# The first main slot's second unit turned by VectorE instead of TensorE

## The chip, the cores and the metric

The kernel runs on one core of one Trainium2 chip. The time is that of one execution on the device in microseconds (us), taken as the median of several runs; before the change it is 705.68 us. The core's engines have queues of their own: TensorE (PE; its weight loads have a row of their own, PEld), VectorE (DVE), ScalarE (ACT), GpSimd (POOL) and SyncE (SP), which only issues transfers here. Each engine takes its queue in order.

## What is computed

Linear attention with exponential features over 8 batches, 8 heads, 576 tokens and 64 columns a head; its output, 4608 tokens of 512 columns, goes through a mixture of eight experts, one expert a token, chosen by a router with a memory along the sequence:

```python
q_p, k_p = phi(q), phi(k)          # exp(x w - max), exp(-(x w - max))
kv = einsum('bhsf,bhsd->bhfd', k_p, v); z = sum(k_p, axis=2)
x = (q_p @ kv) / (q_p @ z + 1e-6)  # heads side by side: 512 columns
...
e = fresh_e if s == 0 or local_gate[b, s] < 0.5 else prev_e
h = maximum(x[b, s] @ w1[e], 0.0)  # 512 -> 1024
out[b, s] = p[e] * (h @ w2[e])     # 1024 -> 512
```

All of it is in 32-bit floats.

## The kernel before

The attention fills the first part of the span. Its tokens are written to DRAM (`xs`), sorted by expert into units of up to 128 tokens, and the experts work on slots: a slot is up to four units of one expert. There are two early slots of three units (`eslots`), which run while the last tokens are being sorted, and then the main slots, the first of which (`by_size[4][0]`) has four units.

For a slot, POOL gathers each unit's tokens from `xs` into an SBUF tile `xg`, tokens on the partitions (`gather_x`, L1302). Layer 1 needs them the other way round, features on the partitions, and in two parts: `xhi`, a rounded copy that ACT casts (L1410), and `xlo`, the rest that DVE subtracts (L1412), both in `parts`. Weights are split the same way: SP loads a piece `wraw`, ACT casts `whi` (L1249), DVE subtracts `wlo` (L1252). A product is three matmuls: high by high, high by low, low by high (L1416 to L1418; the first column block of layer 1 at L1463 takes all high parts of `x` first, and `xlo` last). Layer 1 runs over eight blocks of hidden columns, twelve matmuls each, into PSUM tiles `l1`; layer 2 over the units, 24 matmuls each, into `l2`. ACT scales each unit's result to `y` (L1533), and POOL writes it out by token number (L1537).

A unit is turned in one of two ways:

- `whole` (L1329): four PE transposes into a PSUM tile `tr` (L1335), then `parts` from PSUM. `tokens(..., late=True)` returns one such call a unit.
- `early_rows` (L1380): DVE transposes 32 x 32 blocks of the unit into `z` (L1386), then sixteen copies of 32 partitions x 128 put the blocks in their places, back into `xg` (`places`, four copies for each `j`, L1396), then `parts` from `xg` (`split`). It returns a list of six calls: the blocks, four times places, split. For a slot of four units the copies with odd `j` go to DVE and those with even `j` to ACT.

In the kernel before, the first main slot's unit 0 goes through `early_rows` and units 1, 2 and 3 through `whole`. This happens in layer 2 of the second early slot. `run` gives that layer a list of calls (`later`, second list), one for each pause; the pauses stand behind the first and the third column block of each of its three units. So in order: nothing; unit 0's blocks; `singles` (a step of the plan, in which POOL gathers the list rows of the single units at L937, and unit 0's four places); `parts` of `run` (unit 0's split, unit 1 whole); unit 2 whole; unit 3 whole; and behind the layer the last step of the plan (`more`), which has POOL clear a buffer (L968) and DVE and ACT unpack the list (L970 to L975).

The order of each engine's queue is fixed when the program is built. The framework goes through the instructions with estimated durations of its own and gives a free engine the instruction that is ready; among several, that which was written first. `past(engine)` and `issue_after(x)` add that an instruction comes behind another on its engine: `self.marks` keeps the last marked one, and `parts` marks its subtract on DVE and its cast on ACT. `last_low` is the last weight subtract that was written.

Of the kernel before, what the change touches and what calls it, by code (L numbers as in the profile page):

```python
# [82 lines left out]
class Kernel:  # L83
# [9 lines left out]
    def run(self):  # L93
        nc, tc, A = self.nc, self.tc, self.A
        act, dve = self.act, self.dve
        with ExitStack() as root:
# [38 lines left out]
            n = NBP * NHP * NC  # L135
# [63 lines left out]
            no = lambda: None  # L199
            m = []  # L200

            def ahead(k):
                s = self.by_size[4][0]
                self.gather_x(s, k, self.marks[self.act] if k else None)
                if k == 0:
                    self.coming.append(s)
                if k == 3:
                    m.append(self.early_rows(s, 0))
                    m.extend(self.tokens([s], True)[1:])
            a = [lambda k=k: ahead(k) for k in range(4)]  # L210

            def more():
# [10 lines left out]

            def parts():
                m[0][5]()
                m[1]()
            e, turn = self.eslots[1], []
            for k in range(2):
                turn.append(self.early_rows(e, k))
# [1 line left out]
            def both(*fs):  # L231
                def run():
                    for f in fs:
                        f()
                return run
            u, v = turn
            self.slots(self.eslots, soon=[[no, u[0], u[1], go, u[2], u[3], go, u[4], v[0], go, both(row, v[1]), row,
                                           both(row, v[2]), row, both(row, v[3]), both(row, v[4])],
                                          [no] * 9 + [read, both(a[0], step), a[1], step, a[2], step, a[3]]],
                       later=[[plan_row, u[5], row, row, v[5], 2, row, row, listed], [no, lambda: m[0][0](), singles, parts] + [lambda k=k: m[k]() for k in (2, 3)] + [more]])  # L240
            back.close()
            self.mid.close()
            self.open_rest(root)
# [1136 lines left out]
    def early_rows(self, s, k):  # L1380
        e, x = {}, s["xg"][k]

        def blocks():
            e["z"] = self.back2.tile([128, DM], F32, name="z", tag="kvs", bufs=3)
            with self.tc.issue_after(self.last_low.ins) if s["n"] == 4 else self.past(self.dve):
                self.marks[self.dve] = self.dve.transpose(e["z"].rearrange("p (c t) -> p c t", t=32),  # L1386
                                                          x.rearrange("p (c r) -> p c r", r=32))

        def places(j):
            z, to = e["z"].rearrange("p (a b t) -> p a b t", a=4, b=4), x.rearrange("p (a t) -> p a t", a=4)  # L1390
            g = slice(32 * j, 32 * j + 32)
            for b in range(4):
                q, engine = slice(32 * b, 32 * b + 32), self.dve if s["n"] == 4 and j % 2 else self.act
                with self.past(engine):
                    copy = engine.copy if engine is self.act else engine.tensor_copy
                    self.marks[engine] = copy(to[q, :, g], z[g, :, b, :])  # L1396

        def split():
            hi, lo = self.into(s)
            o = slice(k * 128, k * 128 + 128)  # L1400
            self.parts(s, hi, lo, o, x.rearrange("p (a t) -> p a t", a=4))
        return [blocks] + [lambda j=j: places(j) for j in range(4)] + [split]
# [320 lines left out]
```

## Time and profile before

| | us |
|---|---|
| median of 3 runs | 705.68 |
| lowest, highest | 705.52, 706.1 |
| the profiled execution | 706.37 |
| its span, first to last instruction | 704.6 |

The span is what the profile's views cover; 1.77 us of the profiled execution lie around it. TensorE was granted its full clock throughout (1.000 as the mean). A timeline row gives the start, the duration, the engine, the line, the operation, output<-input with shapes, how many instructions were merged, and in brackets the idle time before it with what ended it. Pipelined matmuls overlap: the pitch from start to start is what one costs.

### The profile page before, as it was taken

To read this page: it belongs to the slowest core of one execution; us is meant where nothing else is said; L and a number is where in the kernel's file an instruction comes from. 1 tells how busy PE (TensorE), PEld (TensorE's weight loads), DVE (VectorE), ACT (ScalarE), POOL (GpSimd) and SP (SyncE) were. 2 spreads that over 40 slices of the span, in tenths; PEclk is the share of its full clock that TensorE was granted. 3 is DMA by queue.
4 is the path that set the end of the run, shared out by engine and by line. 5 is a ranking of instruction groups with operands and counts; after the bars stand their busy time and mean duration, and the time that the engine had idled before them with its cause. 6 is when DMAs were issued, how large, how long until landed. Compare 5 with 4: busy or idle time off the path is not lost. (4 is left out here: it accounts for less than half of the span.)

```text
span 704.6 us, 22501 instructions
## 1 busy us (share of the span) xinstructions
PE 694.4 (99%) x9304; PEld 615.2 (87%) x9304; DVE 480.0 (68%) x941; ACT 416.9 (59%) x916; POOL 269.0 (38%) x534
## 2 busy tenths in 40 slices
PE   7999999999999999999999999999999999999996
PEld 6999999999999999989888988888987888878885
DVE  5798989889998996687757774535466743367230
ACT  4776676777678875843756656627276654256210
POOL 0211100341046576562445575423273836225101
PEclk9999999999999999999999999999999999999999
DMA  7765554555557756064847563445747697372001
GB/s 218 234 185 155 141 149 132 155 162 138 145 155 229 223 175 192 6 187 127 253 163 258 170 208 138 151 165 221 255 165 266 219 357 256 106 250 73 28 16 39
DMA packets 64921, 120.96 MB, mean 172 GB/s; under 512 B 7050, under 2 KB 45130, under 8 KB 64758
## 3 DMA queue, kind: packets, MB, share of 16 engines
q1 hardware_dynamic: 56528, 96.71, 43.4%
q0 software_dynamic: 7968, 22.59, 9.4%
q8 instruction: 74, 1.21, 0.7%
q14 instruction: 31, 0.25, 0.1%
q10 hardware_dynamic: 320, 0.20, 0.1%
HBM read 97.93 MB, written 21.80 MB: 170 GB/s over the span
## 5 line engine op out<-in xcount | busy, mean ns | idle before, releaser
L1252 DVE TENSOR_TENSOR wlo<-wraw,whi 128x1024 fp32r<-128x1024 f32 x80 | 97.0, 1228 | 40.5 <-ACT whi L1249 40.1
L396 ACT ACTIVATE kp<-sb 128x512 f32<-128x512 f32 x144 | 83.3, 623 | 50.4 <-DVE sb L393 46.5
L1416 PE MATMUL l<-whi,hh 128*128 128x512 f32 (+1 forms) x288 | 112.8, 392 | 0.0
L1417 PE MATMUL l<-wlo,hh 128*128 128x512 f32 (+1 forms) x288 | 112.4, 390 | 0.0
L1418 PE MATMUL l<-whi,hl 128*128 128x512 f32 (+1 forms) x288 | 112.3, 390 | 0.0
L1249 ACT CAST whi<-wraw 128x1024 fp32r<-128x1024 f32 x80 | 82.5, 1047 | 47.4 <-PE l L1418 25.8
L1416 PE MATMUL l<-xhi,whi 128*128 128x512 f32 (+5 forms) x308 | 108.4, 352 | 0.0
L1418 PE MATMUL l<-xhi,wlo 128*128 128x512 f32 (+5 forms) x308 | 108.1, 351 | 0.0
L1417 PE MATMUL l<-xlo,whi 128*128 128x512 f32 (+5 forms) x308 | 108.0, 351 | 0.0
L392 DVE TENSOR_REDUCE m<-pj 128x8 f32<-128x1024 f32 (+1 forms) x74 | 88.3, 1193 | 21.9 <-PE pj L385 19.9
L1368 POOL COPY xg<-z 32x128 f32<-32x128 f32 x216 | 79.8, 369 | 48.6 <-DVE z L1356 27.7
L1472 ACT ACTIVATE hh<-l 128x384 fp32r<-128x384 f32 (+4 forms) x88 | 44.8, 509 | 88.6 <-PE l L1463 52.9
L1473 DVE SCALAR_TENSOR_TENSOR hl<-l,hh 128x384 fp32r<-128x384 f32 (+4 forms) x88 | 50.7, 578 | 65.6 <-ACT hh L1472 65.1
L393 DVE TENSOR_TENSOR sb<-pj,m 128x1024 f32<-128x1024 f32 (+1 forms) x74 | 88.5, 1196 | 5.6
L385 PE MATMUL pj<-first,kq 64*128 64x128 f32 x1152 | 86.0, 290 | 4.2 <-DMA first<-in_first 3.6
L1537 POOL DMA_INDIRECT out<-y,p_tokm x31 | 36.6, 1181 | 132.0 <-DVE y L1531 125.7
L517 PE MATMUL nm<-kvs,qp 128*64 128x73 f32 x2304 | 86.3, 227 | 0.1
L420 ACT ACTIVATE qp<-pj 128x512 f32<-128x512 f32 x144 | 78.1, 596 | 9.7 <-PE pj L405 9.0
L385 PEld LDWEIGHTS pj<-first,kq 64*128 64x128 f32 x1152 | 72.0, 192 | 10.2 <-DMA first<-in_first 3.6
L517 PEld LDWEIGHTS nm<-kvs,qp 128*64 128x64 f32 x2304 | 79.1, 137 | 0.5 <-PE nm L517 0.2
L437 PE MATMUL kvp<-v,kp 128*64 128x65 f32 x2048 | 76.5, 226 | 0.1
L437 PEld LDWEIGHTS kvp<-v,kp 128*64 128x64 f32 x2048 | 66.9, 139 | 3.3 <-ACT kp L396 0.2
(282 smaller groups left out, 1071.1 us busy)
## 6 DMA issues: line engine op xcount, KB each, us to landing
wraw<-in_w1h SPq DMA_DIRECT2D x44, 512.0 KB, 5.6
wraw<-in_w2h SPq DMA_DIRECT2D x44, 512.0 KB, 4.5
kq<-in_kqT SPq DMA_DIRECT2D x47, 384.0 KB, 4.0
v<-in_va SPq DMA_DIRECT2D x48, 195.0 KB, 3.3
xs<-xo SPq DMA_DIRECT2D x48, 128.0 KB, 2.8
whi<-in_w2h SPq DMA_DIRECT2D x8, 512.0 KB, 6.9
wlo<-in_w2h SPq DMA_DIRECT2D x8, 512.0 KB, 8.1
xs<-xo SPq DMA_DIRECT2D x16, 192.0 KB, 2.2
```

The costliest lines, as they stand in the source:

```text
L385: self.last_pe = self.pe.matmul((q if j else t)[:, h, i % 2, j, :], kq[r, j, s], self.w2[r], start=True, stop=True)
L392: dve.tensor_reduce(m[:, a:a + n], x[:, s], AX.X, ALU.max, apply_absolute_value=True)
L393: self.last_dve = dve.tensor_sub(to[:, s], x[:, s], m[:, a:a + n].unsqueeze(2).broadcast_to([128, n, 128]))
L396: self.last_act = act.activation(kp[:, :, :, sg, :].rearrange("p c h f -> p h c f"), sb[:, :, :, 0], AF.Exp, scale=1.0 - 2 * sg)
L437: self.pe.matmul(t[r, sg, h], kp[:, h, sg, r], v[:, h], start=first and sg + h == 0, stop=last and sg + h == 2)
L517: self.last_num = self.pe.matmul(e["t"][r, c - c0, k], self.ch[i]["qp"][:, sg, h, q0 + r.start:q0 + r.stop], kvs[:, sg, k], start=sg == 0, ...
L1249: self.act.copy(hi, raw)
L1252: self.last_low = (low or self.dve).tensor_sub(lo[:, c], raw[:, c], hi.bitcast(F32)[:, c])
L1368: self.marks[engine] = copy(to[q, :, g], z[g, :, b, :])
L1416: mm(o, ah, bh, start=first, stop=False)
L1417: mm(o, ah, bl, start=False, stop=False)
L1418: self.last_pe = mm(o, al, bh, start=False, stop=last)
```

## The change

Unit 1 of the first main slot goes through `early_rows` as unit 0 does, and no longer through `whole`. Its blocks are turned in the same pause as unit 0's; its places are called in the pause of `parts`, behind unit 0's split; its split is called in the next pause, ahead of unit 2. For slots of four units the engine of a group of four copies comes from a table of two units by four groups: unit 0 has ACT, DVE, ACT, DVE as before, unit 1 has DVE for the first group and POOL for the other three.

```diff
@@ ahead(k), in run
                 if k == 3:
-                    m.append(self.early_rows(s, 0))
-                    m.extend(self.tokens([s], True)[1:])
+                    m.extend(self.early_rows(s, i) for i in (0, 1))
+                    m.extend(self.tokens([s], True)[2:])
@@ run
             def parts():
                 m[0][5]()
-                m[1]()
+                for f in m[1][1:5]:
+                    f()
+
+            def others():
+                m[1][5]()
+                m[2]()
...
-                       later=[[plan_row, u[5], row, row, v[5], 2, row, row, listed], [no, lambda: m[0][0](), singles, parts] + [lambda k=k: m[k]() for k in (2, 3)] + [more]])
+                       later=[[plan_row, u[5], row, row, v[5], 2, row, row, listed], [no, lambda: [m[k][0]() for k in (0, 1)], singles, parts, others, lambda: m[3](), more]])
@@ early_rows, places(j)
-                q, engine = slice(32 * b, 32 * b + 32), self.dve if s["n"] == 4 and j % 2 else self.act
+                q, engine = slice(32 * b, 32 * b + 32), self.act
+                if s["n"] == 4:
+                    engine = (self.act, self.dve, self.act, self.dve, self.dve, self.pool, self.pool, self.pool)[4 * k + j]
```

## Rows read from the trace of the kernel before

**Rows 1.** The page, part 1: busy us (share of the span) and instructions

```profile
PE 694.4 (99%) x9304; PEld 615.2 (87%) x9304; DVE 480.0 (68%) x941; ACT 416.9 (59%) x916; POOL 269.0 (38%) x534
```

**Rows 2.** Waits of PEld, 326 to 705 us: total, times, longest

```profile
PEld l L1429 <- issue: 8.0, 28, 0.4
...
PEld l L1463 <- ACT whi L1249: 0.8, 1, 0.8
```

**Rows 3.** Timeline of PE around unit 1's transposes (columns: see above)

```profile
336.81 0.39 PE L1417 MATMUL l<-wlo,hh 128*128 128x512 f32 x1
337.04 0.39 PE L1418 MATMUL l<-whi,hl 128*128 128x512 f32 x1
337.27 0.60 PE L1335 MATMUL tr<-first,xg 128*128 128x128 f32 x4
337.63 0.48 PE L1416 MATMUL l<-whi,hh 128*128 128x512 f32 x1
337.94 0.40 PE L1417 MATMUL l<-wlo,hh 128*128 128x512 f32 x1
```

**Rows 4.** Timeline of PE where the first main slot begins

```profile
347.58 1.07 PE L1463 MATMUL l<-xhi,whi 128*128 128x512 f32 x4
```

**Rows 5.** Timeline of ACT, 342 to 347 us

```profile
342.37 0.62 ACT L1410 CAST xhi<-xg 128x512 fp32r<-128x512 f32 x1
342.89 0.58 ACT L1410 CAST xhi<-tr 128x512 fp32r<-128x512 f32 x1
...
344.89 1.08 ACT L1410 CAST xhi<-tr 128x512 fp32r<-128x512 f32 x2
345.84 1.08 ACT L1249 CAST whi<-wraw 128x1024 fp32r<-128x1024 f32 x1
```

**Rows 6.** Timeline of DVE, 333 to 348 us

```profile
333.60 0.69 DVE L1386 STREAM_TRANSPOSE z<-xg 128x512 f32<-128x512 f32 x1
334.23 1.17 DVE L1252 TENSOR_TENSOR wlo<-wraw,whi 128x1024 fp32r<-128x1024 f32 x1
...
342.50 1.23 DVE L1252 TENSOR_TENSOR wlo<-wraw,whi 128x1024 fp32r<-128x1024 f32 x1 [1.09 <-ACT whi L1249]
343.64 0.68 DVE L1412 TENSOR_TENSOR xlo<-xg,xhi 128x512 fp32r<-128x512 f32 x1
...
345.03 1.23 DVE L1252 TENSOR_TENSOR wlo<-wraw,whi 128x1024 fp32r<-128x1024 f32 x1
346.17 1.28 DVE L1412 TENSOR_TENSOR xlo<-tr,xhi 128x512 fp32r<-128x512 f32 x2
```

**Rows 7.** Timeline of POOL, 328 to 346 us

```profile
328.05 0.95 POOL L1302 DMA_INDIRECT xg<-xs,p_tokm  x1 [0.30 <-issue]
...
336.44 1.02 POOL L1537 DMA_INDIRECT out<-y,p_toke  x1 [4.94 <-ACT y L1533]
...
340.29 1.87 POOL L937 DMA_INDIRECT lr<-lst,p_rih  x1 [0.31 <-issue]
344.34 1.04 POOL L1537 DMA_INDIRECT out<-y,p_toke  x1 [2.18 <-ACT y L1533]
```

**Rows 8.** DMA issues, 326 to 332 us: count, median us to landing

```profile
xg<-xs,p_tokm POOLq DMA_INDIRECT x4, 3.6
```

**Rows 9.** Timeline of DVE in the first main slot, 360 to 367 us

```profile
360.63 0.47 DVE L1368 COPY xg<-z 32x128 f32<-32x128 f32 x2
...
365.91 1.23 DVE L1252 TENSOR_TENSOR wlo<-wraw,whi 128x1024 fp32r<-128x1024 f32 x1 [1.80 <-ACT whi L1249]
```

**Rows 10.** Timeline of POOL in the first main slot, 360 to 368 us

```profile
360.09 2.57 POOL L1368 COPY xg<-z 32x128 f32<-32x128 f32 x8 [5.25 <-DVE z L1356]
363.92 3.70 POOL L1368 COPY xg<-z 32x128 f32<-32x128 f32 x8 [1.26 <-DVE z L1356]
```

**Rows 11.** The same groups by tile `z`: ns min/median/max, first to last start

```profile
L1368 POOL COPY xg<-z x8: 281/286/288, 360.1 to 362.4; 32x128 f32<-32x128 f32 x8
...
L1368 POOL COPY xg<-z x8: 283/288/1349, 363.9 to 367.3; 32x128 f32<-32x128 f32 x8
```

## The prediction

> **What bounds the kernel now.** I read the page's busy times first: TensorE (PE) is busy for 99% of the span, every other engine for 68% or less [rows 1]. So a change counts only by what it takes from PE or by what it makes PE wait for. The waits of PE's weight loads from 326 us to the end say whether PE waits anywhere behind the place of the change: 28 short gaps inside one kind of small slot, and single waits of at most 0.8 us [rows 2]. A shift of PE's queue at 337 us will thus travel to the end of the span nearly whole.
>
> Then the timeline of PE. The four transposes of the second unit stand between two matmuls of the second early slot's layer 2 [rows 3]; the same pattern stands twice more, for the third and fourth units. Layer 1 of the first main slot begins on PE at 347.58 without a gap [rows 4]; its products with the low parts `xlo` come eight matmuls of 0.23 later, at 349.4. Its first matmul takes all 512 columns, so it needs `xhi` of all four units. The timelines of the other engines show how much time is left: ScalarE (ACT) casts the first unit's `xhi` at 342.37, the second's, out of PSUM, at 342.89, and has the last two done at 345.97 [rows 5]; VectorE (DVE) has the last `xlo` at 347.45 [rows 6]; GpSimd (POOL) sits idle until 336.44, then issues one output and three gathers up to 342.16, then an output at 344.34 [rows 7].
>
> **What is removed.** From the matmul at 337.04 to the second one behind the transposes at 337.94 are 0.90 us, where two pitches of 0.23 (336.81 to 337.04) would be 0.46 [rows 3]: the four transposes cost PE 0.44 us. Nothing covers that, so it is the gain. Layer 1 of the main slot would be wanted at 347.58 - 0.44 = 347.14. A PSUM tile is no longer used; nothing in the trace waits for one here, and I count it at nothing, whichever way.
>
> **What is added, on DVE.** One block transpose of 0.69 (pitch 0.63), right behind the first unit's at 333.60 [rows 6]. Its data, gathered second of four, are in SBUF by then (landing 3.6 us after issue, before 333) [rows 8]. It pushes the weight subtract at 334.23 and the first unit's copies back by 0.63. Behind those DVE idles until its next weight casts are ready, and the pieces of weights that it splits here belong to the slot that begins at 347, so I cost this at nothing; without that cover it would be 0.63. Four copies (two take 0.47, so 0.235 each [rows 9], 0.94 in all) are written behind the first unit's `xlo`, which ends at 344.32 [rows 6]: they end at 345.3 at the earliest. The second unit's `xhi` can't be cast before, 2.4 us later than now. The cast itself reads SBUF instead of PSUM, 0.62 for 0.58 [rows 5]; it is on ACT, beside PE.
>
> **What is added, on POOL.** Twelve copies, of which the trace has no case here. The nearest rows are eight of the same shape in a main slot: 2.57 us alone, a pitch of 0.32, and 3.70 where a weight subtract of DVE (two SBUF inputs, 365.91) ran beside them [rows 10]; there one copy of 288 ns became 1349 [rows 11]. So a weight subtract that is met costs 1.13.
>
> Where do they stand in POOL's queue? The blocks are ready at 333.60 + 0.63 + 0.69 = 334.92, and POOL idles until 336.44 [rows 7]: about four copies of 0.32 fit in front of the output, if the queue is built in the order in which things become ready. The output and the gathers were written earlier in the program and go first once they are ready, so the other eight copies come behind the last gather: 342.46 + 2.57 = 345.0 at the least. In that stretch DVE runs a weight subtract at 342.50, the first unit's `xlo` (its two inputs are in SBUF too) at 343.64, and another weight subtract, now behind the four copies at about 345.3. The bounds for the end of the copies: 345.0, or below that if more than four come first, and 346.3 + 1.13 + 0.68 + 1.13 = 349.2 with all twelve behind the gathers and all three held. I take eight copies and the first two holds, 345.0 + 1.13 + 0.68 = 346.8, and half of the third, as the pattern of one held copy per subtract is the nearest row: 347.4. The cast of 0.62 then ends at 348.0, against 347.14 wanted: PE waits 0.9.
>
> Queued behind the copies on POOL are the output at 344.34 [rows 7], the singles' list, which needs the buffer of that output, and the gathers for the next slot. They slide by up to 3 us. The next slot begins 192 matmuls of 0.23 us, 44 us, behind the main slot's start. What DVE and ACT do for the singles' list stands in front of their reads of the main slot's PSUM tiles; of those there are four, each filled by 12 matmuls (2.8 us), so three more are there to be filled, 8 us. That is the cover, and I cost the slide at nothing; without it PE would wait up to the 3 us.
>
> A page of the Trainium skill speaks against the change at one point more. Rows first: in the group of eight POOL copies at 360.09 two DVE copies ran at 360.63 [rows 9], and the POOL copies took 281 to 288 ns each [rows 11]; no hold is seen. "SBUF — State Buffer", section "Who interferes with whom", says that VectorE and GpSimd share a port pair as an exclusive lock, and that a VectorE `copy` in a two-port mode takes it too, not only a `tensor_tensor` with two SBUF inputs. By the rows the four DVE copies cost POOL nothing; by that rule they would hold POOL's for four times 0.235.
>
> **The sum.** -0.44 + 0.86 = +0.42 us. The profiled execution took 706.37 (span 704.6 and 1.77 around it), 0.69 more than the median of the three runs; with the change it would take 706.8, and the median 705.68 + 0.42 = 706.1. A difference of 0.2%, 1.41 us, is about what a measurement of this kernel can tell from none, so this is no change.
>
> **The rivals.**
>
> *In time.* The copies end before 346.5: because more than four go in front of the output, or because DVE's subtracts fall between them. For it: POOL idles 4.94 us before the output [rows 7], and bare copies end at 345.0. Against it: the blocks are ready only in the last 1.5 us of that idle time, and three subtracts stand in the way. Then only the gain is left: 705.68 - 0.44 = 705.24.
>
> *ACT held in its queue (slower).* ACT works in order. If the second unit's cast is queued in front of the casts of the third and fourth units (it is written before them), they all wait for POOL. They are now done at 345.97 [rows 5]; behind a cast that ends at 348.0 their 1.08 gives 349.1, and a weight cast between them another 1.08 [rows 5]. PE waits 1.9 to 3.0, the net is +1.5 to +2.6: 707.2 to 708.3. It decides for slower once the last cast ends behind 347.14 + 0.44 + 1.41 = 348.99. For it: that order of writing. Against it: at 345 the other two are ready and the second unit isn't, and a queue built by readiness would let them pass.
>
> *DVE's copies hold POOL's too.* Four holds of 0.235 on top of the forecast: 706.1 + 0.9 = 707.0. Against it stands the 281 to 288 ns [rows 11]. For it: only two DVE copies ran there. The page named above is the one that has this rule.
>
> *The queues come out otherwise further on.* The order of all queues is fixed at build time; a shift of half a microsecond can swap neighbours later. PE has no waits of size there [rows 2], so it can hardly gain, and lose about a microsecond: 704 to 707.5.
>
> *The change doesn't remove what it says.* PE's transposes are issued by one helper, and the second unit's call is dropped from the list; I give that no chance.
>
> **How the numbers follow.** Forecast (a PE wait of 0.3 to 1.5; 705.5 to 706.8) 0.47; in time 0.24; ACT held 0.14; DVE's copies too 0.08; further on 0.07. The likeliest is 706.1. The range from 705.0 to 707.5 holds the forecast, the case in time with a margin of 0.2, the copies' case and the lower third of ACT held; outside are the rest of it and half of the last case, some 0.13. Slower by over 0.2% (above 707.09): ACT held, half of the copies' case, an edge of the forecast and a part of the last: 0.22. Faster by over 0.2% (below 704.27): only a part of the last, 0.03. Within: 0.75.
>
> **What would show it.** Right: eight transposes by PE in front of the main slot instead of twelve; two block transposes back to back at about 333.6; some POOL copies in front of the first output, the others behind the third gather, some of them over 1 us long; ACT idle before the second unit's cast; a gap on PE in front of the first main matmul of about 0.9, released by that cast. Wrong: no gap there (the case in time); the third and fourth units' casts behind the second's (ACT held); or a difference in time that arises behind 370 us.

## The result and the profile after

The changed kernel takes 715.06 us, the median of four runs (714.48 to 716.69), against 705.6 for the kernel before, the median of four runs on the same chip (704.48 to 706.1). The ratio is 1.0134, with an interval from 1.0118 to 1.0149. That is 9.5 us slower, where the prediction had 0.4 us and a range that ended at 707.5. The profiled execution took 714.94 us, with a span of 713.2.

The first view is again the timeline of TensorE (PE); its columns are the start, the time, the engine, line and operation, the tiles, and in brackets the idle time before it with what ended it. Line 1470 of the changed kernel is line 1463 of the one before, 1423 to 1425 are 1416 to 1418. These rows are from the end of the second early slot on.

```profile
345.24 0.39 PE L1425 MATMUL l<-whi,hl 128*128 128x512 f32 x1
353.21 2.04 PE L1470 MATMUL l<-xhi,whi 128*128 128x512 f32 x4 [7.58 <-ACT whi L1254]
355.05 1.91 PE L1470 MATMUL l<-xhi,wlo 128*128 128x512 f32 x4
356.76 1.91 PE L1470 MATMUL l<-xlo,whi 128*128 128x512 f32 x4
358.46 0.63 PE L1423 MATMUL l<-xhi,whi 128*128 128x512 f32 x1
358.89 0.52 PE L1424 MATMUL l<-xlo,whi 128*128 128x512 f32 x1
359.25 0.39 PE L1425 MATMUL l<-xhi,wlo 128*128 128x512 f32 x1
```

Where the main slot began without a gap before [rows 4], PE now stands still for 7.58 us. And the first twelve matmuls behind the stop take 358.46 - 353.21 = 5.25 us. Before they took 350.30 - 347.58 = 2.72. The table of windows says why: the granted clock (the column `PEclk`, the third from the right) is 0.50 there, the lower of the two levels, 1.2 GHz in place of 2.4. It comes back to 1.00 in the stretch from 358.5 to 360 (0.78 as the mean): the matmuls from 359.25 on have the pitch of before. Each row gives the stretch, its length, then the busy time and the instructions of PE, PEld, DVE, ACT and POOL.

```profile
340.00:345.50 5.50, 5.50 (x29) 4.33 (x26) 3.99 (x7) 3.49 (x5) 4.58 (x4) 1.00 0.85 289
345.50:353.20 7.70, 0.13 (x1) 0.02 (x1) 1.43 (x3) 2.08 (x4) 1.53 (x3) 0.72 0.41 109
353.20:356.00 2.80, 2.79 (x7) 2.22 (x8) 2.40 (x4) 0.81 (x3) 0.69 (x2) 0.50 0.26 97
356.00:358.50 2.50, 2.50 (x8) 1.92 (x7) 0.18 (x1) 0.69 (x3) 1.89 (x3) 0.50 0.81 197
358.50:360.00 1.50, 1.50 (x7) 1.23 (x6) 0.60 (x1) 0.60 (x1) 1.20 (x2) 0.78 1.01 393
360.00:362.00 2.00, 2.00 (x10) 1.64 (x9) 0.09 (x1) 0.24 (x1) 0.45 (x1) 1.00 1.00 410
```

Who held PE? The timeline names the weights, which came last by a little. Followed back one step on ScalarE (ACT), where rows 5 had no wait, they stand in its queue behind the casts of `xhi`, and those behind a wait of 7.61 us for GpSimd (POOL). VectorE (DVE) subtracts `xlo` behind that cast.

```profile
342.93 0.58 ACT L1417 CAST xhi<-tr 128x512 fp32r<-128x512 f32 x1
351.12 0.62 ACT L1417 CAST xhi<-xg 128x512 fp32r<-128x512 f32 x1 [7.61 <-POOL xg L1403]
351.64 0.58 ACT L1417 CAST xhi<-tr 128x512 fp32r<-128x512 f32 x1
352.12 1.05 ACT L1254 CAST whi<-wraw 128x1024 fp32r<-128x1024 f32 x1
```

POOL itself (the answer to rows 7):

```profile
333.40 5.39 POOL L1403 COPY xg<-z 32x128 f32<-32x128 f32 x11 [3.50 <-DVE z L1391]
339.07 1.70 POOL L1544 DMA_INDIRECT out<-y,p_toke  x1 [0.28 <-POOL xg L1403]
341.08 1.82 POOL L942 DMA_INDIRECT lr<-lst,p_r  x1 [0.31 <-issue]
343.20 0.90 POOL L942 DMA_INDIRECT lr<-lst,p_rih  x1 [0.30 <-issue]
344.40 1.28 POOL L942 DMA_INDIRECT lr<-lst,p_rih  x1 [0.31 <-issue]
350.80 0.29 POOL L1403 COPY xg<-z 32x128 f32<-32x128 f32 x1 [5.11 <-DMA lr<-lst,p_rih]
```

Eleven of the twelve copies went in front of the output. The twelfth, 0.29 us long, stands behind the output and the three gathers of the singles' list, and the row says that it waited 5.11 us until the last gather had landed. It doesn't read what that gather brings: the gathers fill `lr`, the copy moves a block from `z` to `xg`. Its line of code asks for no such order; in the built program its wait is on the completion of every one of the four transfers that stand before it in POOL's queue. Whether the chip needs that wait, or only the program asks for it, no run here shows.

A trace could have told this beforehand. The tile view of `z` in the kernel before, POOL's copies alone, gives the idle time in front of them by what ended it. This group isn't among the rows ahead of the prediction, and I hadn't read it as a price:

```profile
L1368 POOL COPY xg<-z x216: 279/287/1349, 360.1 to 643.9; 32x128 f32<-32x128 f32 x108
...
  DVE z L1356: 27.7, 16
...
  DMA out<-y,p_tokm: 8.4, 4
```

Four times, 8.4 us in all, a POOL copy had waited for an output, which it has no business with either.

**An account by stages.** Single runs of the kernel before spread by 4 us (704.19 to 708.6 in 22 runs), and the profiles show where: the second early slot, which lies in front of the change's effects, began anywhere from 311.19 to 314.23 in the twelve profiled executions. So each trace is cut at the first matmul of a slot, the rows of PE that follow (before, then after; the main slot's own rows are in rows 4 and above):

```profile
312.80 0.87 PE L1463 MATMUL l<-xhi,whi 128*128 128x384 f32 x4
422.98 1.08 PE L1463 MATMUL l<-xhi,whi 128*128 128x512 f32 x4
502.30 0.74 PE L1463 MATMUL l<-xhi,whi 128*128 128x320 f32 x4
```

```profile
311.19 0.87 PE L1470 MATMUL l<-xhi,whi 128*128 128x384 f32 x4
431.52 1.08 PE L1470 MATMUL l<-xhi,whi 128*128 128x512 f32 x4
510.84 0.74 PE L1470 MATMUL l<-xhi,whi 128*128 128x320 f32 x4
```

Stage A runs from the second early slot to the first main slot (347.58 - 312.80 = 34.78 before), stage B from there over two main slots (422.98 - 347.58 = 75.40), stage C over the next two (79.32). Each figure is from the one profiled execution of its kernel. The table has the difference to the kernel before in each stage, their sum, and what the timed runs gave by their ratio to the kernel before on the same chip (the interval in us). The runs below stand in it too.

| kernel | A | of it, layer 2 | B | C | sum | timed |
|---|---|---|---|---|---|---|
| changed kernel | +7.24 | +7.25 | +2.91 | 0 | +10.2 | +9.5 (8.3 to 10.5) |
| e1_last_dve | +0.72 | +0.65 | +0.30 | 0 | +1.0 | +2.0 (1.0 to 3.0) |
| e2_first | +0.83 | +0.50 | +0.78 | +0.51 | +2.1 | +2.8 (1.7 to 3.8) |
| e3_behind | +4.94 | +4.57 | +1.96 | 0 | +6.9 | +7.5 (5.6 to 9.4) |
| e4_no_turn | -0.22 | -0.50 | 0 | 0 | -0.2 | +0.1 (-1.1 to 1.3) |
| e5_busy | +6.84 | +6.84 | +0.12 | 0 | +7.0 | +7.6 (6.1 to 9.1) |
| e6_swap | +0.16 | +0.03 | +0.85 | +0.75 | +1.8 | +2.0 (0.8 to 3.2) |
| e7_list | +0.34 | +0.35 | +0.10 | 0 | +0.4 | +0.7 (-0.4 to 1.8) |
| e8_late | +2.18 | +1.62 | +0.09 | 0 | +2.3 | +2.2 (0.9 to 3.5) |
| e9_all | +0.12 | +0.13 | +0.12 | 0 | +0.2 | -0.1 (-1.4 to 1.1) |
| e10_all_act | -0.28 | -0.27 | +0.12 | 0 | -0.2 | +0.5 (-0.6 to 1.7) |

The column "of it, layer 2" counts stage A only from the first layer 2 matmul of the second early slot, 18.11 us before the main slot in the kernel before:

```profile
329.47 0.39 PE L1416 MATMUL l<-whi,hh 128*128 128x512 f32 x1
```

The part of stage A ahead of that matmul lies before everything that the change or an edit moves. It took 16.66 to 16.80 us in eight of the executions, but 16.95 in e4_no_turn, 17.00 in e2_first, 17.04 in e3_behind and 17.23 in e8_late, where PE's weight load stands still for 0.3 to 0.6 us near 319.5 (in three of the four for DVE's `hl`). So the column is the better measure of what an edit does to stage A.

The sum lies inside the timed interval in every line. For the changed kernel, A is the stop less the transposes, 7.58 - 0.44 = 7.14 and 0.10 more; B is the lower level, 5.25 - 2.72 = 2.53 in the first twelve matmuls and the rest in the next ones.

### The profile page after: what moved, and what is told of

Same layout as the page of the kernel before. It is cut to its first block, busy times and chain, and to the rows that moved or that the text cites. A ratio compares the mean times of both kernels' runs of the same rounds, so it can differ in the third digit from the quotient of the medians.

```text
span 713.2 us, 22512 instructions
## 1 busy us (share of the span) xinstructions
PE 695.6 (98%) x9300; PEld 615.3 (86%) x9300; DVE 483.4 (68%) x946; ACT 417.8 (59%) x916; POOL 277.8 (39%) x546
```

## The experiments

In the code and in the expectations the units count from 0, so that unit 1 is the second one, which the change turns, and unit 2 the third. The theory: one copy behind transfers of POOL's own costs the stop, and the stop costs TensorE its level. The rivals: that POOL's copies are too many or too slow wherever they stand; that the lower level is only a companion; that the change has further costs in ACT's and DVE's queues or later on.

**The twelfth copy on DVE.**

```
...
-                     engine = (self.act, self.dve, self.act, self.dve, self.dve, self.pool, self.pool, self.pool)[4 * k + j]
+                     engine = (self.act, self.dve, self.act, self.dve, self.dve, self.pool, self.pool, self.pool)[4 * k + j] if (k, j, b) != (1, 3, 3) else self.dve
```

> The changed kernel with one of the sixteen copies moved: the twelfth of GpSimd's, the last, goes to VectorE; eleven stay on GpSimd. Theory A (one copy behind the gathers): the whole loss comes from that one copy, which stands behind one output and three gathers in GpSimd's queue and waits for them to land (5.1 us idle in the trace), and from the lower TensorE clock behind the gap. Then it is gone: 705.2 us (the kernel before at 705.7, less 0.44 for four transposes), no gap on TensorE in front of the first main slot. Theory B (GpSimd's work as such: twelve copies beside VectorE's subtracts are too slow, the mechanism of the forecast): eleven copies are nearly the same work, at least 713. Theory C (the second unit's cast holds ScalarE's queue wherever its copies are made): 708 or more.

708.34 us (707.06 to 708.55), ratio 1.0028 (1.0014 to 1.0043). One copy of 0.29 us moved, and 6.5 of the 7.24 us of stage A are gone, and 2.6 of the 2.91 of stage B with them. The eleven copies that stay cost little. But the time is not theory A's 705.2; it lies where theory C had it. What is left is a stop of 0.98 us, which the row puts down to DVE and not to ACT's queue (e6_swap, below, tries that):

```profile
347.95 1.17 PE L1470 MATMUL l<-xhi,whi 128*128 128x512 f32 x4 [0.98 <-DVE xlo L1419]
```

**All twelve in front.** POOL's copies are issued at a higher priority, so that none stands behind the output.

```
- with self.past(engine):
+ with self.past(engine), self.tc.high_priority() if engine is self.pool else nullcontext():
```

> The changed kernel with all twelve copies on GpSimd, but given priority over what else is ready, so that all twelve stand in front of the output and the three gathers in its queue. Only the place of one copy differs. Theory A: 705.2 us, no gap on TensorE; the output and the gathers 0.3 us later. Theory B: the same work on the same engine, so 714 to 716. Theory C: 708 or more.

708.94 us (706.86 to 710.28), ratio 1.0039 (1.0024 to 1.0054). Again the big stop is gone, without taking a copy from POOL: it is the place, not the engine. In the built program the queues of PE, ACT and DVE are those of the changed kernel; only POOL's differs, by the place of the twelfth copy. But 2 to 3 us remain (again the time of theory C), and they lie in three stages. In the main slot PE's weight loads waited 0.6 us for ACT's `hh` and 0.4 us for DVE's `hl`, where its layer 2 begins, 26.9 us behind its start (375.86):

```profile
375.34 0.39 PE L1425 MATMUL l<-whi,hl 128*128 128x512 f32 x1
375.86 0.50 PE L1423 MATMUL l<-whi,hh 128*128 128x512 f32 x1
```

The singles' list comes late too, on ACT 6.2 us behind the slot's start, where the kernel before had it 2.8 us behind (350.39). But the `hh` that are queued right behind it made PE wait for nothing. What is late at 375.86 is the work on the next slot's tokens, which stands on ACT and DVE between the `hh` and `hl`, and it is late because POOL's gathers of those tokens stand behind the list's memset, which had waited for an output to land:

```profile
353.96 0.30 POOL L973 MEMSET y<- 32x256 f32 x1 [4.26 <-DMA out<-y,p_toke]
358.63 0.95 POOL L1307 DMA_INDIRECT xg<-xs,p_tokm  x1 [0.30 <-issue]
```

The last of these gathers goes 9.67 us behind the slot's start, against 6.31 in the kernel before. The runs are in that order: where it goes at 8.2 us or earlier and the clock holds, stage B has at most 0.12 more than before; at 9.33 (e1_last_dve) it has 0.30, at 9.67 0.78, at 9.73 (e6_swap) 0.85.

**All twelve behind.** POOL's copies wait for the issue of the last gather.

```
- ins = pool.indirect_dma_start(...
+ ins = self.last_lr = pool.indirect_dma_start(...
...
- with self.past(engine):
+ with self.tc.issue_after(self.last_lr.ins) if engine is self.pool else self.past(engine):
```

> The changed kernel with all twelve copies behind the last of the three gathers in GpSimd's queue. Theory A: the first of them waits for the landing as the one copy did, and then twelve at a pitch of 0.32 us follow instead of one, 3.5 us more: 717 to 719 us, and a gap on TensorE of about 11 us. Theory B (no wait for a landing, only work and VectorE's holds): the copies end at 346.3 to 349.2, so 706 to 709.

713.34 us (711.83 to 714.53), ratio 1.0106 (1.0079 to 1.0133): slower than before, but less so than the changed kernel, which neither number had foreseen. POOL shows why. With no copies in front, the last gather goes 28.2 us behind the start of the second early slot (340.94 - 312.78), where the changed kernel has 33.2. The first copy still comes only 5.7 us behind that gather's start, and the twelve take 5.16, so the last is done 0.9 us earlier than in the changed kernel. The row names no transfer for this wait; in the built program it is again on the completion of the four in front. But ACT had cast the third and the fourth unit by then, and only one cast stood between the copies and PE.

```profile
340.94 1.59 POOL L942 DMA_INDIRECT lr<-lst,p_rih  x1 [0.31 <-issue]
346.64 5.16 POOL L1403 COPY xg<-z 32x128 f32<-32x128 f32 x12 [4.11 <-issue]
```

PE's stop is 4.92 us, ended by the cast of the second unit. So the price of the place isn't a fixed one: it is the landing of the last transfer in front, and whatever had delayed that transfer.

**The unit not turned at all.** The block transpose and the copies of the second unit are left out, which shows what the removal on PE is worth by itself.

```
  if k == 3:
      m.extend(self.early_rows(s, i) for i in (0, 1))
+     m[1][0:5] = [no] * 5
```

> The changed kernel without the turning of the second unit: its block transpose and its sixteen copies are left out, and its cast reads the rows as they were gathered. It shows what taking four transposes from TensorE is worth when nothing is put in their place: 705.2 us if the 0.44 us arrives at the end, 705.7 if it is lost on the way. If it were slower than 706, the loss would lie in the new order of the calls and not in the copies at all.

706.78 us (704.64 to 707.76), ratio 1.0002 (0.9985 to 1.0019). Stage A is 0.22 us shorter, half of the 0.44. But it holds a wait of 0.3 us for DVE's `hl`, which the kernel before doesn't have:

```profile
319.86 0.19 PEld L1424 LDWEIGHTS l<-xhi,whi 128*128 128x128 f32 x1 [0.31 <-DVE hl L1481]
330.39 0.39 PE L1424 MATMUL l<-whi,hh 128*128 128x512 f32 x1
```

It lies ahead of layer 2, where nothing has been edited. From layer 2 on the stage is 0.50 us shorter (348.00 - 330.39 = 17.61 against 18.11): the whole of the 0.44 arrives. By timing it can't be told from nothing.

**TensorE kept at work.** Thirty matmuls into a tile that nobody reads are put in the stop of the changed kernel.

```
+ def busy():
+     w = self.by_size[4][0]["w"][0][0]
+     t = self.pskv.tile([128, 512], F32, name="idle", tag="kvp")
+     for k in range(30):
+         with self.here():
+             self.last_pe = self.pe.matmul(t, w[:, 0:128], w[:, 0:512], start=True, stop=True)
...
-     ... others, lambda: m[3](), more]])
+     ... others, lambda: m[3](), both(more, busy)]])
```

> The changed kernel, with 30 matmuls of 128x128x512 added that TensorE works through while it would otherwise stand still ahead of the first main slot (they write a PSUM tile that nobody reads; nothing else is touched). Theory A (the still stretch also costs TensorE its level: the twelve first-layer matmuls behind it took 5.25 us against 2.72 before, and the slot's next ones about 0.4 more): the twelve take 2.7 to 2.9 us, the granted clock from 346 to 360 is 1.00, the stretch from the first matmul of the main slot to the first of the next is 43.5 us and not 46.4, and the time falls by 2.5 to 2.9 us, to about 712.3. Theory B (the clock is a mere companion, the twelve matmuls were slow because their operands came late): they still take about 5 us and the time stays at 715. In both, the first matmul of the main slot still comes some 42 us behind the slot before it.

713.4 us (712.31 to 713.91), ratio 1.0108 (1.0087 to 1.0129). The first main matmul still comes 41.62 us behind the slot before it (42.02 in the changed kernel), on operands just as late, but the level holds and stage B is 75.52 us, not 78.31:

```profile
346.81 6.96 PE L234 MATMUL idle<-whi 128*128 128x512 f32 x30
354.18 1.17 PE L1477 MATMUL l<-xhi,whi 128*128 128x512 f32 x4 [0.41 <-ACT whi L1261]
355.19 1.08 PE L1477 MATMUL l<-xhi,wlo 128*128 128x512 f32 x4
```

So 2.8 us of the loss are TensorE's level; work that has no use at all gains them back. In time the two kernels differ by 1.7 us between medians, less than the stage, and their intervals overlap a little.

**DVE's order.** e1_last_dve, with unit 2's subtract ahead of unit 1's.

```
  def others():
-     m[1][5]()
      m[2]()
+     m[1][5]()
```

> As e1_last_dve (the twelfth copy on VectorE), but VectorE subtracts unit 2's part ahead of unit 1's. Theory A (what was left of the stop ahead of the main slot, 0.98 us, is VectorE's order: the PSUM tile of unit 2 is given back only behind unit 1's subtract): the stop shrinks by one subtract, 0.6 us, to 0.3 to 0.4 us; from the slot before to the main slot 34.9 us against 35.5 in e1_last_dve and 34.8 before; the time falls by 0.6 us. Theory B (unit 1's cast, which comes at 345.4, or the weights set the stop): the stop stays at 0.9 to 1.0 us and the time at that of e1_last_dve.

707.66 us (705.87 to 710.01), ratio 1.0028 (1.0012 to 1.0045). The stop before the main slot falls from 0.98 to 0.36 us, stage A from +0.72 to +0.16 (from layer 2 on, +0.65 to +0.03), as expected: the PSUM tile of the third transpose, which the main slot's first matmul is to write, was given back a subtract too late (its reader is the third unit's `xlo`, which the row names). But the time doesn't fall, since stages B and C go up by 0.55 and 0.75: the main slot comes 0.6 us sooner, POOL's gathers for the next slot only 0.2, and the waits are those of e2_first.

```profile
PEld l L1423 <- ACT hh L1479: 0.6, 1, 0.6
PEld l L1425 <- DVE hl L1480: 0.4, 1, 0.4
```

**The singles' list in a tile of its own.** e2_first, but the list is unpacked in a tile that the output isn't still reading.

```
- t = (self.back2.tile([128, DM], F32, name="z", tag="kvs", bufs=3) if engine is dve else
+ t = (self.back2.tile([128, DM], F32, name="z", tag="kvs", bufs=3) if engine is dve or n == ONES + DUALS else
       self.mx2.tile([128, DM], F32, name="y"))
```

> As e2_first (all twelve copies ahead of the output), but the singles' list is unpacked in a tile of its own, so that its memset no longer waits for the second unit's output to land (4.26 us idle on GpSimd in e2_first). Theory A (the waits inside the main slot, 0.6 us for a ScalarE hh and 0.4 us for a VectorE hl, come of this list, whose copies stand ahead of the hh casts on ScalarE's queue at 355.2): ScalarE's list copies come at 349 to 352, the waits inside the main slot go, from the first matmul of the main slot to the first of the next 43.5 us against 44.3 in e2_first, and the time falls by 0.8 us or a little more. Theory B (the list has no part in them): 44.3 us as before, and the time of e2_first.

706.99 us (705.54 to 708.56), ratio 1.001 (0.9995 to 1.0025). Stages B and C fall back to +0.10 and 0 from +0.78 and +0.51, and the waits inside the slots are gone. So the list is their cause, but not by the way of theory A: ACT's list copies come at 353.96, not at 349 to 352, as the gathers' landing takes the place of the output's, and that is still 5.7 us behind the slot's start (6.2 in e2_first). What moves is POOL. No memset waits there, and the last gather for the next slot goes 5.35 us behind the slot's start, not 9.67:

```profile
353.62 0.95 POOL L1307 DMA_INDIRECT xg<-xs,p_tokm  x1 [0.30 <-issue]
```

The lag is handed on to the third main slot on the same queue: in the second one a group of POOL's copies waited 4.48 us for an output in e2_first and 1.08 in e7_list, and the last of the gathers behind them went 73.9 us behind the first main slot's start, not 67.0. That path is read from the rows; no run tries it alone.

**The gathers behind the twelfth copy.**

```
  def singles():
-     more()
      ...
  def others():
+     more()
```

> The changed kernel, with the three gathers of the singles' list issued behind the twelfth copy; GpSimd's queue is now eleven copies, the output, the twelfth copy, the second output, the gathers. Theory A (the twelfth copy waited for the landing of the gathers in front of it): it now waits for the output alone, issued at about 339 and landed 3.6 to 5 us later, so it goes at 343 to 344.5; no more than about 1 us of stop is left ahead of the main slot (as in e1_last_dve) and the TensorE level holds; the list comes later still, so 0.8 to 1.5 us of waits inside the main slot; the time is 707 to 709. Theory B (a copy that stands behind any transfer of GpSimd's waits some 5 to 7 us, whichever it is, or the copy is held by something else than the gathers): the copy goes behind 346, the stop is 3 us or more, and the time is 711 to 715.

708.36 us (707.47 to 709.05), ratio 1.0031 (1.0013 to 1.0049). The time is in the range of theory A, three of its numbers are not:

```profile
340.91 1.02 POOL L1544 DMA_INDIRECT out<-y,p_toke  x1 [0.28 <-POOL xg L1403]
345.93 1.33 POOL L1403 COPY xg<-z 32x128 f32<-32x128 f32 x1 [3.99 <-DMA out<-y,p_toke]
```

The copy now waits for the output, 5.0 us from its start, and then takes 1.33 us beside a weight subtract of DVE (345.88), so the stop is 1.97 us and not 1. The waits in the main slot didn't come; the last gather for the next slot goes 8.16 us behind its start. What follows stands: the copy waits for the last transfer in front of it, whichever that is.

**The cures together**: the edits of e6_swap and e7_list, and the twelfth copy on DVE (e9_all, below) or on ACT (e10_all_act, with `self.act` as the last word).

```
-                     engine = (self.act, self.dve, self.act, self.dve, self.dve, self.pool, self.pool, self.pool)[4 * k + j]
+                     engine = (self.act, self.dve, self.act, self.dve, self.dve, self.pool, self.pool, self.pool)[4 * k + j] if (k, j, b) != (1, 3, 3) else self.dve
...
```

> The three cures together: the twelfth copy on VectorE (as in e1_last_dve), unit 2's subtract ahead of unit 1's (e6_swap), the singles' list in a tile of its own (e7_list). Theory A (the change's loss is the sum of these three and of TensorE's level, and nothing else): from the slot before to the main slot 34.9 us as in e6_swap (34.8 before), in the main slot 43.5 to 43.6 (44.4 in e6_swap, 43.5 before), behind it 111.2; the time is that of the kernel before, within 0.2% (705.2 to 706.9). Theory B (something else of the change costs 1 to 2 us, say in front of these stages): the three stretches come out so, and yet the time stays 0.2 to 0.3% above that of before.

> As e9_all, with the twelfth copy on ScalarE, which stood still for 0.5 to 0.6 us ahead of unit 1's cast because VectorE's five copies came late. Theory A (VectorE's copies now hold unit 1's cast and by it the main slot): four copies in place of five, so the cast comes 0.25 us earlier, and the 0.36 us of stop that e6_swap had left shrinks to 0.1; 34.6 us from the slot before to the main slot, time 705 to 706.5. If VectorE's subtracts behind the copies set the stop, it shrinks by the same 0.25. Theory B (ScalarE's queue is as full as VectorE's: the copy, 0.3 us, moves the 0.68 us activation and the weights behind it): 34.9 us or more, time as e9_all or later.

e9_all: 706.32 us (704.18 to 708.47), ratio 0.9998 (0.998 to 1.0015). e10_all_act: 706.34 us (704.67 to 709.46), ratio 1.0007 (0.9991 to 1.0024). Both are the kernel before, within what can be measured (1.1 and 1.7 us at the upper ends); the loss is thus the sum of these causes and nothing else of size. Between the two, stage A differs by 0.40 us: with five copies DVE had held the cast of the second unit and by it the main slot (a stop of 0.50), with four it starts within 0.1 us of the last matmul's end.

```profile
345.76 1.17 PE L1470 MATMUL l<-xhi,whi 128*128 128x512 f32 x4
```

Even so, this best arrangement is worth 0.2 us in the sum of its stages (0.28 in A), and its time isn't below that of the kernel before. None of the versions beats it.

## Why the prediction was wrong, step by step

**A shift of PE travels to the end.** Right: of the changed kernel's 10.2 us in stages A and B none is given back in C or behind it.

**The transposes, -0.44.** Right: e4_no_turn has -0.50 from layer 2 on. It decided nothing.

**POOL's queue: the step that failed.** I took four copies in front of the output and eight behind the last gather, on the ground that the output and the gathers were written earlier and go first. Eleven went in front. That by itself would have been good news, as the rival "in time" had it. The failure is in the bounds of the next sentence: the copies behind the gathers were to begin at 342.46, 0.30 behind the end of the last gather's issue in the kernel before, so the latest end was 349.2. Two things are wrong in that start. An issue that is over isn't a transfer that has landed: the twelfth copy began at 350.80, 5.11 us behind the last issue's end. And that issue didn't end where it had: counted from the start of the second early slot it ended at 34.49 us (345.68 - 311.19) and not at 29.36 (342.16 - 312.80), because eleven copies, 5.39 us, now stood in front of the output and the gathers. About half of the lateness is the one and half the other; e3_behind, with no copy in front, has the landing without the second half and, even with all twelve copies behind it, a stop of only 4.92. A PE wait of 0.86 us became 7.58. The kernel before had the row for it (8.4 us of POOL copies that waited for an output), and I read the copies' durations in that view but not their waits.

**ACT held in its queue.** The second half of this rival is what happened: the third and fourth units' casts were to wait behind the second's. One did (351.64), the other had passed (342.93); the weight cast that the rival had in between came too (352.12), and PE waited for its end. Its price, 1.5 to 2.6, started from a cast that ended at 348.0 and so had the same error in it.

**The weight subtracts.** About right: two of the eleven copies met one, and they took 1.14 and 1.19 us, the others 0.29 to 0.32. So each cost 0.85 to 0.90 us, where I had 1.13 from the eight-copy rows.

**DVE's part at nothing.** Nearly: 0.40 us between e9_all and e10_all_act is what one copy too many on DVE costs there, once the big stop is gone. The hold on POOL that I worked out from the Trainium skill ("SBUF — State Buffer", "Who interferes with whom": an exclusive lock between VectorE and GpSimd, which a VectorE `copy` in a two-port mode takes too) isn't borne out: the eight POOL copies that began between 334.6 and 336.9, beside DVE's, took 286 to 319 ns. It was DVE's copies that got longer, 316 ns in the median of eight against 220 before. A lock that POOL takes first would do that too; no run here tells.

```profile
L1396 DVE COPY xg<-z x8: 217/220/303, 335.6 to 337.5; 32x128 f32<-32x128 f32 x8
L1403 DVE COPY xg<-z x8: 215/316/323, 334.5 to 338.3; 32x128 f32<-32x128 f32 x8
```

**A PSUM tile counted at nothing.** Wrong by 0.6 once the big stop is gone: e1_last_dve against e6_swap, 0.98 to 0.36 us. In the kernel before nothing waits for such a tile. Once the second unit's subtract comes late, the third's is queued behind it on DVE, and its tile with it.

**The slide of POOL's later work at nothing, for four PSUM tiles, 8 us.** Wrong in the runs that let it show: 0.5 to 0.75 us in each of stages B and C of e2_first and e6_swap, gone in e7_list. The cover that I named held: the reads behind the list made PE wait for nothing. It wasn't the cover of the gathers for the next slot, which I had in the same list; where the last of them went 9.3 us or more behind the main slot's start, PE waited at the beginning of its layer 2. In the changed kernel itself it costs nothing: there the stop gives them the time, and the last one goes 6.29 us behind the start.

**What no term had.** TensorE's level. I priced a wait of PE at its length. The wait of 7.58 us cost 2.8 us more behind its end; the one of 4.92 in e3_behind, 1.96 us more in stage B.

## What to carry to other kernels

Before an engine's copy is put on a queue that also issues transfers, look up in the trace what such copies have waited for there: if it is a transfer that they don't touch, their place among the issues counts for more than their number, and one copy behind the last issue costs a whole landing, and whatever the copies in front have delayed that issue by. Price a stop of TensorE by its length and by the matmuls behind it, at the level that the clock view shows. And where a gain is under half a microsecond and single runs spread by several, cut the traces at marks on the bounding engine and compare stage by stage.

## What the runs showed of the hardware

- TensorE's granted clock went from 1.00 to 0.50 in the stop of 7.58 us (2.4 to 1.2 GHz) and stayed there for the first 5.25 us of work behind it. It was 0.50 behind the stop of 4.92 us in e3_behind too. A stop of 1.97 us (e8_late) left it at 1.00, and cost no more than its length and 0.09 us in stage B.
- Six DVE copies of 32x128 blocks beside POOL copies of the same shape took 287 to 323 ns, against 220 in the median without them, while the POOL copies stayed within 0.04 us of their bare time.
- A POOL copy of 0.29 us that met a weight subtract of DVE (two inputs in SBUF) took 1.14 and 1.19 us.
- An indirect transfer of POOL's, on whose completion the built program makes the next POOL copy wait, held that copy from the start of its issue for 5.0 us (the output, in e8_late) to 6.4 us (the last gather, 344.40 to 350.80).
